# Two transformer layers on one core: interleaved MLP chains, two-bank exponentials in the last attention block, plain score maxima listed one unit later

## The chip, the cores and the metric

The kernel runs on one core of one Trainium2 chip. The metric is the device time of one execution in microseconds (us). The kernel before the change has a median of 3666.82 us in 3 runs (3660.86 to 3669.71).

## The reference

Two layers are computed on `x` of 2048 rows and 640 columns, in fp32. Each layer is an attention block (32 heads of 20) and an MLP (640 to 1536 to 640, squared relu), both with a layernorm in front and a residual behind. Both layers use the same weights.

```python
def _A_ref(x, wqkv, wo):
    qkv = (x @ wqkv).reshape(B, S, 3, H, Dh).transpose(2, 0, 3, 1, 4)
    q, k, v = qkv[0], qkv[1], qkv[2]
    scores = jnp.einsum("bhqd,bhkd->bhqk", q, k) * (Dh ** -0.5)
    p = _softmax(scores, axis=-1)
    o = jnp.einsum("bhqk,bhkd->bhqd", p, v)
    return o.transpose(0, 2, 1, 3).reshape(B, S, D) @ wo

def _B_ref(x, w1, b1, w2, b2):
    h = jnp.einsum("bsd,df->bsf", x, w1) + b1
    r = jnp.where(h > 0, h, 0)
    return jnp.einsum("bsf,fd->bsd", r * r, w2) + b2

x = x + _A_ref(_layernorm(x), wqkv, wo)
x = x + _B_ref(_layernorm(x), w1, b1, w2, b2)
x = x + _A_ref(_layernorm(x), wqkv, wo)
x = x + _B_ref(_layernorm(x), w1, b1, w2, b2)
```

## The kernel before

Every fp32 product is made of three products of rounded halves (`THREE`: high by high, high by low, low by high). A layer has three stages, and the program of each engine is written out by hand: engines work through their lists strictly in order and wait on semaphores, so the place of an instruction in its list decides what stands behind it while it waits.

**qkv.** The rows are taken in four blocks `tb` of 512. The projections to q and k come in 40 units: one unit is one chain of matmuls (L321 in `product`), worked as two half chains on the upper and the lower 64 rows of the array, 30 matmuls a unit. A finished chain is copied out by ACT, split into halves by POOL (`split_on_pool`), stored to DRAM (`d_qk`), and loaded again in the layout of the heads (`load_k`, `load_q`). The softmax needs the maximum of each row of scores. It is found beforehand, by matmuls of q with k (L473, `by_queries`) whose results DVE reduces (L485, "plain" maxima, listed in `PLAIN`) or whose pairs of key blocks are combined by ACT and DVE (L494 and L502, listed in `DOUBLE`, with the tiles `kd` of differences of keys). As many of these as fit are put between the projection matmuls; the rest is done in the attention stage. After each unit the counter `n` decides whether the loads of a group are issued (`tiles`) and whether its maxima are put on the list `groups`, from which `following` takes them.

**attention.** There are 32 blocks `t` of 512 queries by 4 heads, each with 16 units (`NKT`), a unit being 128 keys. A unit has four score matmuls into the four banks of `ps_st` (L555), four exponentials by ACT (L562, one bank of 512 columns each), and the product with v (L567, `pv`), whose eight matmuls (four heads, two passes) add to bank 7. Banks 4 to 6 belong to the maxima (L473). The strings in `ORDERS` give the order: a and b are scores, m and n maxima, V is `pv` of the oldest unit. In the last block no maxima are left, so only a, b and V do anything there.

**mlp.** After the output projection, each of four row blocks `qb` goes through two halves `fh` of the hidden width: six chains of the first product (L285, 512 columns wide) give six tiles `h` by ACT relu with bias (L1147), DVE square (L1148), ACT cast to the high half (L255) and DVE difference for the low half (L256). Then eight chains of the second product (L285, 320 columns) of 18 matmuls each run through the six tiles in order, and DVE adds each result to its rows (L1167). The line that builds a chain of the second product:

```python
                    chain(dst[:, :HALF], [
                        (hs[f % 6][:, hx, i * P : (i + 1) * P], w_2.piece(at_2(f, hw, hf)))
                        for f in range(fh * 6, fh * 6 + 6)
                        for hx, hw in THREE
                    ])
```

Of the kernel before, what the change touches and what calls it, by code (L numbers as in the profile page):

```python
# [10 lines left out]
AF = mybir.ActivationFunctionType  # L11
# [5 lines left out]
P = 128  # L17
# [22 lines left out]
def tile_layers(  # L40
# [11 lines left out]
    nc = tc.nc  # L52
# [17 lines left out]
    def dma(eng, dst, src):  # L70

        if dst.dtype == F32R:
            dst = dst.bitcast(F32)
        if src.dtype == F32R:
            src = src.bitcast(F32)
        eng.dma_start(dst, src)  # L76
# [4 lines left out]
    banks = psum.tile([P, 8, 512], F32, tag="banks", name="banks")  # L81
# [17 lines left out]
    ps_all = Ring(0, 1, 2, 3, 4, 5, 6, 7)  # L99
# [102 lines left out]
    w_2 = Split("w2", HALF, NF * 4)  # L202

    def at_2(f, hw, hf):

        return (((f // 6) * 2 + hf) * 6 + f % 6) * 2 + hw
# [75 lines left out]
    def chain(dst, pairs):  # L282
        last = len(pairs) - 1
        for n, (a, b) in enumerate(pairs):
            nc.tensor.matmul(dst, a, b, start=(n == 0), stop=(n == last))  # L285
# [387 lines left out]
    def qkv(first, x_src, rest):  # L673
# [41 lines left out]
        def tiles(x):  # L715
            g, qb, c = x
            for c in [c] if c in range(4) else [c, 2 * "de".index(c)]:
                if (g, c) not in k_t:
                    if c in range(4):
                        load_k(g, c, g > 1)  # L720
                    else:
                        load_kd(g, c)
            if g * NQB + qb not in q_t:
                load_q(g * NQB + qb)
# [159 lines left out]
        for j in range(len(chains)):  # L884
            if j < len(UNITS):
                while UNITS[min(j + 1, len(UNITS) - 1)][0] not in xt_:
                    step_rest()
                run(early, j)
            while min(at_now) < (j + 1) * N if j + 1 == len(chains) else at_now[0] < (j + 1) * N:
                for r in range(2):  # L890
                    if not insert(r):
                        work_on(r)
                now["pe"] += 0.235 if j < len(UNITS) else 0.155
                state["n"] += 1
                if state["n"] % 4 == 0 and not state["turn"]:
                    step_rest()
            if first:
                w_qk.save_full(1)
                w_v.save_full(1)
            if j < len(UNITS):  # L900
                run(late, j)
                later(1)
            n = j - 2
            if 1 < n < NQB * FIRST + 2:
                b, step = divmod(n - 2, 4)
                have, new = groups, PLAIN[b][step // 2]
                if step % 2:
                    have.extend(new)
                    soon[:] = [y for y in soon if y not in new]
                elif new:  # L910
                    tiles(new[0])
                    soon.append(new[0])
                if step == 2 and DOUBLE[b][0]:
                    tiles(DOUBLE[b][0][0])
                    soon.append(DOUBLE[b][0][0])
            if n in (10, 13, 17):
                b = n // 4 - 1
                double.extend(DOUBLE[b][0] + DOUBLE[b][1])
                coming[:] = [y for y in coming if y not in double]
                soon[:] = [y for y in soon if y not in double]  # L920
# [20 lines left out]
    def attention(first, x_src, first_rows):  # L941
# [59 lines left out]
        def op(o):  # L1001
            if o in "ab":
                par = "ab".index(o)
                i, p = divmod(st_n[par], 2)
                if i >= last:
                    return
                st_n[par] += 1
                if i > state["begun"]:
                    state["begun"] = i
                    begin(i)  # L1010
                score(i // NKT, i % NKT, 2 * p + par, es_of.setdefault(i, {}))
            elif o in "mn":
# [12 lines left out]
                smax(sm_ring, t, p, sub, c, par)  # L1025
                if n == ends[t] and min(sm_n) > n:
                    over.add(t)
                    if t * NKT > state["begun"] + 2 * NKT:
                        del q_t[t]
            else:  # L1030
                i = state["done"]
                if i >= last or min(st_n) < 2 * (i + 1):
                    return
                t, u = divmod(i, NKT)
                if u == 0:
                    state["acc"] = banks[:, 7, :]
                pv(state["acc"], t, u, es_of.pop(i))
                state["done"] += 1
                if u == NKT - 1:
                    steps = finish(t, state["acc"])  # L1040
                    split.update((i + j, f) for j, f in zip((4, 6, 7, 9, 11, 12), steps))
                t = rows["next"]
                if rows["at"] is not None:
                    if state["begun"] >= rows["at"]:
                        mrows_load(t)
                        rows.update(next=t + 1, at=None)
                elif t in over and t in q_t and state["begun"] >= (t - 2) * NKT + 4:
                    mrows_max(t)
                    mrows(t)
                    rows["at"] = state["begun"] + 2  # L1050

        def pairs():

            n, i = min(sm_n), state["begun"] + 1
            most = max(
                [8 * (e + 1 - n) / max(t * NKT - 5 - i, 1) for t, e in ends.items() if e >= n],
                default=0,
            )
            state["debt"] += most
            n = min(max(round(state["debt"]), 12), 16)  # L1060
            state["debt"] -= n
            return n

        for o in "abab":
            op(o)
        while state["done"] < last:
            for o in ORDERS[pairs()]:
                op(o)
        q_t.clear()
        k_t.clear()  # L1070
        v_t.clear()
# [60 lines left out]
    def mlp(qb, xnt, x_mid, x_dst, side):  # L1132

        xs = []
        for fh in range(2):
            hs = []
            for f in range(fh * 6, fh * 6 + 6):
                dst = ps_all("pu")
                chain(dst, [
                    (w_1.piece(f * 10 + hw * KD + k), xnt[k][:, hx, :])  # L1140
                    for k in range(KD)
                    for hw, hx in THREE
                ])
                if qb == NQB - 1:
                    w_1.past(f * 10 + 9)
                r = xtile("r")[:, :QB]
                nc.scalar.activation(r, dst, AF.Relu, bias=b1_t[:, f : f + 1])  # L1147
                nc.vector.tensor_mul(r, r, r)  # L1148
                h = slot([P, 2, QB], F32R, "h")
                split_to(h[:, 0, :], h[:, 1, :], r)  # L1150
                hs.append(h)
                if fh == 0 and f in (1, 2, 3, 4):
                    x = row_tile(x_mid, qb * 4 + f - 1)
                    nc.gpsimd.tensor_add(x, x, b2_t)
                    xs.append(x)
                side()
            for hf in range(2):
                c = slice(hf * HALF, (hf + 1) * HALF)
                for i in range(4):
                    dst = ps_all("y")  # L1160
                    chain(dst[:, :HALF], [
                        (hs[f % 6][:, hx, i * P : (i + 1) * P], w_2.piece(at_2(f, hw, hf)))
                        for f in range(fh * 6, fh * 6 + 6)
                        for hx, hw in THREE
                    ])
                    x = xs[i]
                    nc.vector.tensor_add(x[:, c], dst[:, :HALF], x[:, c])  # L1167
                    if fh == 1 and hf == 1:
                        r0 = (qb * 4 + i) * P
                        dma(nc.sync, x_dst[r0 : r0 + P, :], x)  # L1170
                    side()
            if fh == 0 and qb == NQB - 1:
                w_2.past(at_2(5, 1, 1))

# [169 lines left out]
```

## Time and profile before

| what | before |
|---|---|
| median of 3 runs | 3666.82 us (3660.86 to 3669.71) |
| the profiled execution's own time | 3667.64 us |
| its span, first to last instruction | 3665.0 us |
| mean granted TensorE clock | 0.996 |
| busy share of PE, DVE, ACT, POOL | 99%, 74%, 72%, 22% |
| layer 1: qkv, attention, output projection and mlp | to about 321, 1415 and 1845 us |
| layer 2: the same | to about 2152, 3241 and 3665 us |

A busy PE in this profile is not PE at its peak: the ends of matmuls are modelled, and an instruction whose start is held back can still leave the engine counted as busy. Waits are therefore read from the distance between starts and from the weight loads (PEld), which stand in the same list as the matmuls and wait for the same semaphores.

### The profile page before, as it was taken

The page shows a single profiled execution, that of the slowest core. Times are in us where ns is not written, and L with a number is a line of the kernel's source. Part 1 is how long each engine was busy: PE and PEld are TensorE (multiplying, and loading weights), DVE is VectorE, ACT ScalarE, POOL GpSimd, SP SyncE. Part 2 cuts the span into 40 slices and gives each one's busy share as a digit, 9 for nine tenths or more (in the row PEclk, how much of TensorE's full clock was granted, in tenths as well). Part 3 has the DMA queues.
Part 4 walks back from the last instruction along what each step waited for, and adds up shares of the span by engine and source line. Part 5 has one row for each costly group of instructions (what it writes and reads, how often), then busy time and mean ns, then how long its engine had stood idle before and what let it go on. Part 6 is the DMA issues. An engine that isn't in the chain of part 4 may idle for free.

```text
span 3665.0 us, 67658 instructions
## 1 busy us (share of the span) xinstructions
PE 3627.8 (99%) x25770; PEld 2165.3 (59%) x25770; DVE 2725.3 (74%) x5039; ACT 2645.5 (72%) x5199; POOL 819.1 (22%) x909
## 2 busy tenths in 40 slices
PE   8999999999999999999999999999999999999999
PEld 6896343333334336899878963333343433378998
DVE  7877999999999982344567779999999999723443
ACT  2778999999999994122217789999999999941221
POOL 6530433221221120111154202211211212101110
PEclk9999999999999999999999999999999999999999
DMA  7875555323221137411367652232232121373111
GB/s 262 286 233 170 167 149 155 102 68 79 56 49 44 50 104 241 155 44 44 101 229 244 219 151 75 69 78 55 71 76 58 47 52 42 110 258 132 44 51 36
DMA packets 255260, 426.50 MB, mean 116 GB/s; under 512 B 60444, under 2 KB 107292, under 8 KB 254936
## 3 DMA queue, kind: packets, MB, share of 16 engines
q1 hardware_dynamic: 254120, 419.83, 37.2%
q8 instruction: 202, 3.31, 0.4%
q10 hardware_dynamic: 816, 2.36, 0.2%
q14 instruction: 122, 1.00, 0.1%
HBM read 262.20 MB, written 159.88 MB: 115 GB/s over the span
## 4 chain that ended last, share of the span: by engine, by line
PE 95%; DVE 2%; ACT 1%; DMA 1%; POOL 1%; issue 0%; SPq 0%; ACTq 0%; DVEq 0%; POOLq 0%
PE banks L567 28%; PE banks L285 21%; PE banks L555 20%; PE banks L473 16%; PE banks L321 10%; DMA q<-d_qk 1%; DVE h L256 1%; PE banks L1121 0%; DVE r L1148 0%; ACT h L255 0%; PE banks L392 0%; DVE mx L485 0%; ACT r L1147 0%; DVE bst L243 0%; SPq L76 0%
## 5 line engine op out<-in xcount | busy, mean ns | idle before, releaser
L562 ACT ACTIVATE e<-banks 128x512 f32<-128x512 f32 x4096 | 2113.5, 604 | 66.1 <-PE banks L555 5.5
L485 DVE TENSOR_REDUCE mx<-banks 128x1 f32<-128x512 f32 x3068 | 1927.3, 684 | 218.2 <-PE banks L473 144.6
L473 PE MATMUL banks<-k,q 60*128 60x512 f32 x3583 | 1248.6, 429 | 12.4 <-DMA q<-d_qk 10.5
L555 PE MATMUL banks<-q,k 62*128 62x512 f32 x4096 | 1152.7, 435 | 0.9 <-ACT rl L494 0.5
L567 PE MATMUL banks<-e,vg 128*32 128x512 f32 x8192 | 1092.9, 605 | 0.0
L555 PEld LDWEIGHTS banks<-q,k 62*128 62x128 f32 x4096 | 600.1, 185 | 695.9 <-ACT e L562 664.2
L473 PEld LDWEIGHTS banks<-k,q 60*128 60x128 f32 x3583 | 583.0, 185 | 299.4 <-DVE mx L485 216.0
L502 DVE CUSTOM_DVE_ANT_0 rl<-banks,rl 128x512 f32<-128x512 f32 x515 | 335.8, 689 | 105.6 <-PE banks L473 93.7
L321 PE MATMUL banks<-xnT,wqk 64*128 64x512 f32 x2400 | 385.9, 399 | 3.5 <-DVE xnT L256 1.2
L567 PEld LDWEIGHTS banks<-e,vg 128*32 128x32 f32 x8192 | 161.6, 108 | 357.7 <-issue 332.3
L285 PE MATMUL banks<-w,h 128*128 128x320 f32 x2304 | 358.8, 312 | 7.5 <-DVE h L256 4.3
L285 PEld LDWEIGHTS banks<-w,h 128*128 128x128 f32 x2304 | 340.9, 189 | 17.0 <-DVE h L256 8.7
L494 ACT ACTIVATE rl<-banks 128x512 f32<-128x512 f32 x519 | 275.1, 597 | 96.8 <-PE banks L473 96.0
L285 PE MATMUL banks<-xnT,w 128*128 128x512 f32 x1440 | 330.0, 389 | 0.0
L1147 ACT ACTIVATE r<-banks,b_t 128x512 f32<-128x512 f32 x96 | 66.1, 689 | 360.0 <-PE banks L285 357.8
L321 PEld LDWEIGHTS banks<-xnT,wqk 64*128 64x128 f32 x2400 | 291.1, 189 | 36.5 <-ACT r L262 2.0
L285 PEld LDWEIGHTS banks<-xnT,w 128*128 128x128 f32 x1440 | 269.5, 188 | 55.1
L267 POOL CAST mr<-nt 128x32 fp32r<-128x32 f32 x64 | 13.4, 209 | 1172.7 <-DVE nt L528 1172.7
L611 POOL TENSOR_TENSOR few<-few,minus_t 128x16 f32<-128x16 f32 x62 | 179.8, 2900 | 199.6 <-DMA few<-d_s 199.6
L321 PE MATMUL banks<-wv,xnT 64*128 64x320 f32 x1920 | 198.9, 307 | 1.8 <-ACT mark_t L323 1.8
L1167 DVE TENSOR_TENSOR x<-banks,x 128x320 f32<-128x320 f32 x128 | 62.9, 492 | 183.3 <-PE banks L285 183.0
L255 ACT CAST xnT<-banks 128x512 fp32r<-128x512 f32 x70 | 39.9, 588 | 212.9 <-PE banks L1121 132.0
(77 smaller groups left out, 2104.1 us busy)
## 6 DMA issues: line engine op xcount, KB each, us to landing
q<-d_qk SPq DMA_DIRECT2D x248, 240.0 KB
d_qk<-ev SPq DMA_DIRECT2D x80, 512.0 KB
k<-d_qk SPq DMA_DIRECT2D x152, 240.0 KB
x<-d_x SPq DMA_DIRECT2D x88, 320.0 KB
d_qk<-ev SPq DMA_DIRECT2D x80, 256.0 KB
d_o<-ot SPq DMA_DIRECT2D x248, 80.0 KB
ot<-d_o SPq DMA_DIRECT2D x38, 512.0 KB
d_v<-v SPq DMA_DIRECT2D x32, 512.0 KB
```

What stands on the lines that cost most here:

```text
L285: nc.tensor.matmul(dst, a, b, start=(n == 0), stop=(n == last))
L321: m = nc.tensor.matmul(ch["dst"][:, :width], *pair, start=first, stop=last)
L473: nc.tensor.matmul(dst, q_t[t][b : b + 60, p, sub * P : (sub + 1) * P], k_t[t // NQB, c][b : b + 60, p, :], start=True, stop=True,)
L485: nc.vector.tensor_reduce(maxima(t)[:, 2 * par + p, sub, c : c + 1], dst, axis=AX.X, op=ALU.max)
L494: nc.scalar.activation(res, dst, AF.Relu)
L502: nc.vector.tensor_tensor_reduce(out=r, in0=dst, in1=r, scale=1.0, scalar=LEAST, op0=ALU.add, op1=ALU.max, accum_out=maxima(t)[:, 2 * par ...
L555: nc.tensor.matmul(dst, k_t[t // NQB, kt // 4][b : b + 62, p, (kt % 4) * P : (kt % 4 + 1) * P], q_t[t][b : b + 62, p, :], start=True, stop ...
L562: nc.scalar.activation(es[p][:, par, :], dst, AF.Exp, scale=SCALE)
L567: nc.tensor.matmul(acc[32 * h : 32 * h + 32, :], v_t[t // NQB, kt // 8][:, kt % 8, 32 * h : 32 * h + 32], es[p][:, par, :], start=(kt == 0 ...
L611: nc.gpsimd.tensor_tensor(few, few, minus_t, op=ALU.pow)
L1147: nc.scalar.activation(r, dst, AF.Relu, bias=b1_t[:, f : f + 1])
L1167: nc.vector.tensor_add(x[:, c], dst[:, :HALF], x[:, c])
```

## The change

Three edits that do not touch each other.

In the mlp, the first two chains of each second product are opened together: five sixths of the first, five sixths of the second, the last sixth of the first, the last sixth of the second, then both additions. The other six chains are as before.

In the last attention block of each layer (the units from `wide = last - NKT` on), `both_heads` writes the scores of a pair of heads into two neighbouring banks out of 0 to 5 and takes both with one exponential of 1024 columns. The order there is written anew: `pv` of a unit, then the second pair of the next unit and the first pair of the one after it.

In qkv, the maxima of a plain group are put on `groups` one unit later than before; the loads are issued where they were.

```diff
@@ qkv @@
-            if 1 < n < NQB * FIRST + 2:
-                b, step = divmod(n - 2, 4)
-                have, new = groups, PLAIN[b][step // 2]
-                if step % 2:
-                    have.extend(new)
-                    soon[:] = [y for y in soon if y not in new]
-                elif new:
-                    tiles(new[0])
-                    soon.append(new[0])
-                if step == 2 and DOUBLE[b][0]:
+            b, step = divmod(n - 2, 4)
+            if step % 2 == 0 and 0 <= b <= NQB:
+                if b < NQB and PLAIN[b][step // 2]:
+                    tiles(PLAIN[b][step // 2][0])
+                    soon.append(PLAIN[b][step // 2][0])
+                new = PLAIN[b][0] if step and b < NQB else PLAIN[b - 1][1] if not step and b else []
+                groups.extend(new)
+                soon[:] = [y for y in soon if y not in new]
+                if step and b < NQB and DOUBLE[b][0]:
                     tiles(DOUBLE[b][0][0])
                     soon.append(DOUBLE[b][0][0])
@@ attention @@
-                if i >= last or min(st_n) < 2 * (i + 1):
+                if i >= last or i < last - NKT and min(st_n) < 2 * (i + 1):
...
+        def both_heads(p):
+
+            i = state["wide"]
+            t, kt = divmod(i, NKT)
+            if p == 0 and i > state["begun"]:
+                state["begun"] = i
+                begin(i)
+            es = es_of.setdefault(i, {})
+            es[p] = weights[len(e_n) % len(weights)]
+            e_n.append(t)
+            state["bank"] = (state["bank"] + 2) % 6
+            dst = banks[:, state["bank"] : state["bank"] + 2, :]
+            for par in range(2):
+                b = 64 * par
+                nc.tensor.matmul(
+                    dst[:, par, :],
+                    k_t[t // NQB, kt // 4][b : b + 62, p, (kt % 4) * P : (kt % 4 + 1) * P],
+                    q_t[t][b : b + 62, p, :],
+                    start=True,
+                    stop=True,
+                )
+            nc.scalar.activation(es[p], dst, AF.Exp, scale=SCALE)
+            if p:
+                state["wide"] += 1
...
+        wide = last - NKT
+        state.update(wide=wide, bank=2)
+        spare = 0
+        while state["done"] < wide:
+            for o in ORDERS[pairs()]:
+                if o in "ab" and st_n["ab".index(o)] == 2 * wide:
+                    spare += 1
+                    if spare in (2, 4):
+                        both_heads(spare // 2 - 1)
+                else:
+                    op(o)
+        assert min(sm_n) == len(todo) and spare == 4
+        both_heads(0)
         while state["done"] < last:
-            for o in ORDERS[pairs()]:
-                op(o)
+            op("V")
+            for p in (1, 0):
+                if state["wide"] < last:
+                    both_heads(p)
@@ mlp @@
+            f0 = fh * 6
+
+            def part(dst, hf, i, fs):
+                for f in fs:
+                    for hx, hw in THREE:
+                        nc.tensor.matmul(
+                            dst[:, :HALF],
+                            hs[f][:, hx, i * P : (i + 1) * P],
+                            w_2.piece(at_2(f0 + f, hw, hf)),
+                            start=(f == 0 and (hx, hw) == THREE[0]),
+                            stop=(f == 5 and (hx, hw) == THREE[-1]),
+                        )
...
+            first_two = [ps_all("y") for _ in range(2)]
+            for fs in (range(5), (5,)):
+                for i in range(2):
+                    part(first_two[i], 0, i, fs)
+            for i in range(2):
+                add(first_two[i], 0, i)
             for hf in range(2):
-                c = slice(hf * HALF, (hf + 1) * HALF)
-                for i in range(4):
+                for i in range(0 if hf else 2, 4):
                     dst = ps_all("y")
...
+                    part(dst, hf, i, range(6))
+                    add(dst, hf, i)
```

Three places in PE's list show what moves; they are told here in the order of the argument. The first is in the last attention block of layer 1, near its end; `e` are the tiles of exponentials, `q`, `k`, `vg` those of the queries, keys and values. Before:

```order
L555 MATMUL banks<-q_14199,k_5403 128x512 x4
L567 MATMUL banks<-e_4758,vg_14075 32x512 x2
L567 MATMUL banks<-e_4757,vg_14075 32x512 x2
L555 MATMUL banks<-q_14199,k_5403 128x512 x4
L567 MATMUL banks<-e_4754,vg_14075 32x512 x2
L567 MATMUL banks<-e_4753,vg_14075 32x512 x2
```

The same place after the change:

```order
L1065 MATMUL banks<-q_14198,k_5402 128x512 x4
L567 MATMUL banks<-e_4750,vg_14074 32x512 x2
L567 MATMUL banks<-e_4749,vg_14074 32x512 x2
L1065 MATMUL banks<-q_14198,k_5402 128x512 x4
L567 MATMUL banks<-e_4752,vg_14074 32x512 x2
L567 MATMUL banks<-e_4751,vg_14074 32x512 x2
```

The rows look alike, but a row of four scores is another one: before, it is the whole of unit i+1, ahead of the product of unit i; now it is the second pair of unit i and the first pair of unit i+1, so the second pair of a unit stands behind the product of the unit before it.

The second place is the start of the second product in layer 1, on PE; `h` are the hidden tiles in the order of `f`, and the last of the six is h_16244 before and h_16211 now. Before, the first chain and the start of the second:

```order
L285 MATMUL banks<-w_15941,h_16196 128x320 x3
L285 MATMUL banks<-w_15941,h_16220 128x320
L285 MATMUL banks<-w_15943,h_16220 128x320
L285 MATMUL banks<-w_15941,h_16220 128x320
L285 MATMUL banks<-w_15943,h_16244 128x320 x3
L285 MATMUL banks<-w_15937,h_16119 128x320 x3
```

Now, from the same tile of the first chain to the last tile of both:

```order
L1201 MATMUL banks<-w_15908,h_16187 128x320
L1201 MATMUL banks<-w_15904,h_16086 128x320 x3
L1201 MATMUL banks<-w_15904,h_16115 128x320
L1201 MATMUL banks<-w_15906,h_16115 128x320
L1201 MATMUL banks<-w_15904,h_16115 128x320
L1201 MATMUL banks<-w_15906,h_16139 128x320 x3
L1201 MATMUL banks<-w_15908,h_16163 128x320 x3
L1201 MATMUL banks<-w_15908,h_16187 128x320
L1201 MATMUL banks<-w_15910,h_16187 128x320
L1201 MATMUL banks<-w_15908,h_16187 128x320
L1201 MATMUL banks<-w_15910,h_16211 128x320 x6
```

Fifteen matmuls of the second chain have moved ahead of the first use of the last tile, and nothing else stands between.

The third place is on PE in the qkv stage of layer 2, where the first group of maxima starts; `xnT` and `wqk` are the operands of the projections. Before, it stands behind the 180th projection matmul of the stage:

```order
L321 MATMUL banks<-xnT_18605,wqk_18682 128x512
L321 MATMUL banks<-xnT_18605,wqk_18719 128x512
L473 MATMUL banks<-k_19119,q_19122 128x512 x4
L321 MATMUL banks<-xnT_18535,wqk_18719 128x512
L321 MATMUL banks<-xnT_18535,wqk_18682 128x512
```

Now it stands behind the 210th:

```order
L321 MATMUL banks<-xnT_18572,wqk_18695 128x512
L321 MATMUL banks<-xnT_18572,wqk_18658 128x512
L473 MATMUL banks<-k_19086,q_19089 128x512 x4
L321 MATMUL banks<-xnT_18502,wqk_18658 128x512
L321 MATMUL banks<-xnT_18765,wqk_18620 128x512
```

One unit, 30 matmuls, has moved ahead of the group. Counted through the list in the same way, the later plain groups of layer 2 start at matmul 270 and 336 (before 240 and 306), the first use of a `kd` tile moves from 390 to 396, and in layer 1 the first group moves from 180 to 222 and the first `kd` from 398 to 390. Layer 1 fits as many maxima between its projections as before, layer 2 eight matmuls of maxima fewer, which are done in its attention stage.

More of the change, by code (lines that the diff above doesn't have):

```diff
@@ L1156, in mlp, with add @@
                 side()
+            f0 = fh * 6
[9 more added lines that the diff above has]
+                        )
+            def add(dst, hf, i):
+                c = slice(hf * HALF, (hf + 1) * HALF)
+                x = xs[i]
+                nc.vector.tensor_add(x[:, c], dst[:, :HALF], x[:, c])
+                if fh == 1 and hf == 1:
+                    r0 = (qb * 4 + i) * P
+                    dma(nc.sync, x_dst[r0 : r0 + P, :], x)
+                side()
+            first_two = [ps_all("y") for _ in range(2)]
[4 more added lines that the diff above has]
+                add(first_two[i], 0, i)
             for hf in range(2):
-                c = slice(hf * HALF, (hf + 1) * HALF)
-                for i in range(4):
+                for i in range(0 if hf else 2, 4):
                     dst = ps_all("y")
[L1161 to L1171, printed above, removed]
+                    part(dst, hf, i, range(6))
+                    add(dst, hf, i)
             if fh == 0 and qb == NQB - 1:
```

## The prediction

> **What bounds the kernel now.** I read the page first: the engines' busy time, then the chain that ended last.
>
> ```profile
> PE 3627.8 (99%) x25770; PEld 2165.3 (59%) x25770; DVE 2725.3 (74%) x5039; ACT 2645.5 (72%) x5199; POOL 819.1 (22%) x909
> PE 95%; DVE 2%; ACT 1%; DMA 1%; POOL 1%; issue 0%; SPq 0%; ACTq 0%; DVEq 0%; POOLq 0%
> ```
>
> TensorE is the bound nearly everywhere, so an edit is worth what PE waits at its place, or what it newly makes PE wait. All three edits touch PE's list, each in another stage, so I read each stage by itself: the table by stage around the last attention block, then timelines of PE and ACT.
>
> ```profile
> 1380.00:1390.00 10.00, 10.00 (x61) 3.29 (x60) 0.69 (x1) 9.94 (x20) 0.00 (x0) 1.00 0.35 114
> ...
> 1384.48 1.07 PE L567 MATMUL banks<-e,vg 128*32 128x512 f32 x8
> 1385.48 1.05 PE L555 MATMUL banks<-q,k 62*128 62x512 f32 x4
> ...
> 1386.01 0.60 ACT L562 ACTIVATE e<-banks 128x512 f32<-128x512 f32 x1
> ...
> 1414.55 0.15 PEld L567 LDWEIGHTS banks<-e,vg 128*32 128x32 f32 x6 [0.56 <-ACT e L562]
> ```
>
> In the stretch 1380 to 1390 of the first of these tables DVE has nothing left (0.69) and ACT is busy 9.94 of 10.00: the last block is held by exponentials. Its first product starts at 1384.48 and its last at 1414.55: 15 steps in 30.07 us, 2.00 us a unit.
>
> The profiled execution took 3667.64 us, 0.8 above the median of the runs shown (3666.82); the sum is made against it. About 0.3% (11 us) is what a measurement can tell from no change.
>
> **The change part by part. The mlp chains.** The weight loads show the wait, in the table of waits and in PE's timeline:
>
> ```profile
> PEld banks L285 <- DVE h L256: 8.7, 17, 1.6
> PEld banks L285 <- ACT h L255: 7.1, 15, 2.1
> ...
> 1552.98 2.94 PE L285 MATMUL banks<-w,h 128*128 128x320 f32 x17
> 1556.10 3.05 PE L285 MATMUL banks<-w,h 128*128 128x320 f32 x19 [0.17 <-DVE h L256]
> ...
> 1559.58 2.65 PE banks L285 x18
> ...
> 1770.86 2.57 PE L285 MATMUL banks<-w,h 128*128 128x320 f32 x15
> 1775.26 0.56 PE L285 MATMUL banks<-w,h 128*128 128x320 f32 x2 [1.83 <-ACT h L255]
> 1775.99 5.32 PE L285 MATMUL banks<-w,h 128*128 128x320 f32 x24 [0.17 <-DVE h L256]
> ...
> 1776.20:1779.70 3.50, 3.50 (x15) 3.50 (x15) 1.49 (x4) 0.00 (x0) 0.74 (x2) 0.51 0.33 96
> ```
>
> 18 matmuls run in 2.65 us, 0.147 each. In an ordinary first chain the eighteenth starts 1556.10 - 1552.98 = 3.12 after the first instead of 17 x 0.147 = 2.50: 0.6 lost, on the high half of the last tile and then on its low half. There are 32 such waits, two in each of the 16 first chains (2 layers, 4 row blocks, 2 halves), 8.7 + 7.1 = 15.8 us together. The dearest one is followed by a stretch at 0.51 of the clock: 24 matmuls take 5.32 instead of 3.5, 1.8 more. At stake: 17.6 us. The edit puts 15 matmuls, 2.2 us, in front of the first use of the last tile. The longest wait, 2.1, fits under that; behind it the low half comes 0.73 after the high one (1775.99 against 1775.26), so some 0.5 stays there. **Gain 17 us, 15 to 17.6.** What hides the conversions afterwards is the second chain; without it the 0.7 of each chain would be back. The additions of the two chains come together, a chain later, into a ring of eight banks with six free: nothing.
>
> **The plain maxima.** PE waits for q tiles in DRAM:
>
> ```profile
> PE banks L473 <- DMA q<-d_qk: 11.1, 4, 4.1
> ...
> 42.95 7.55 DMA q<-d_qk
> 80.27 7.84 DMA q<-d_qk
> 1870.18 4.87 DMA q<-d_qk
> 1894.29 5.29 DMA q<-d_qk
> ...
> 50.50:60.00 9.50, 9.41 (x52) 7.19 (x54) 5.46 (x9) 2.06 (x4) 5.04 (x6) 0.71 0.84 288
> 1875.00:1882.00 7.00, 6.81 (x43) 5.86 (x45) 5.81 (x10) 0.14 (x1) 2.62 (x3) 0.76 0.95 347
> 1900.00:1908.00 8.00, 8.00 (x46) 6.81 (x47) 5.36 (x9) 0.67 (x2) 0.81 (x2) 0.63 1.00 316
> ```
>
> The four waits end 4.9 to 7.8 us after the issue of the load. Three are plain groups; the short one, at 88.1, is for a `kd` group, whose list the edit leaves alone. Behind each long wait the clock falls: 9.5 x 0.29 + 7 x 0.24 + 8 x 0.37 = 7.4 us more. At stake: 11.1 + 7.4 = 18.5. Thirty projection matmuls, a whole unit, now cover each group; the waits themselves should go. But the loads that follow keep their own pace, and PE reaches them earlier. In layer 2:
>
> ```profile
> 1904.13 0.78 SPq L76 DMA_DIRECT2D q<-d_qk  x2
> ...
> 1895.60 0.82 PE L321 MATMUL banks<-xnT,wqk 64*128 64x512 f32 x4
> 1899.71 0.76 PE L473 MATMUL banks<-k,q 60*128 60x512 f32 x1 [3.29 <-DMA q<-d_qk]
> ...
> 1914.71 0.39 PE L473 MATMUL banks<-kd,q 60*128 60x512 f32 x1
> ...
> 1880.62 5.57 DVE mx L485 x9
> ```
>
> The third plain group would start at 1896.4 instead of 1899.71. From there to the first `kd` maximum it was 84 projection matmuls in 15.0 us, 12.0 without the slow clock; now it is 60, so 8.6: PE is there at 1905.0. Its q pair was issued at 1904.13. SP takes it in order behind stores of evictions that now run about 4.3 earlier (the first stall of 3.2 and part of its slow stretch, for which DVE, on the chain from 1880.62, had become the pace), so 1899.8, and lands up to 7.84 later, the longest of the four rows, since the DMA share there is 1.00: 1907.7. A wait of 2.7 comes back, with even odds of a slow window of 1.7. Of the 11.1 at stake in layer 2 (3.2 + 3.3 + 1.7 + 3.0, rounded) 1.7 was hidden behind DVE, 2.7 + 0.9 come back: 5.8. In layer 1, 4.1 + 2.8 = 6.9 are at stake and the 80.27 load returns about 2 in the same way: 5. **Gain 10.8 us**; 18.5 if no later load is late, 5 if they all are. Eight maxima matmuls move from one PE-bound stage to another: nothing.
>
> **The last block.** In the order now, the product of unit i stands ahead of the second pair of scores of unit i+1, whose exponential the product of unit i+1 waits for. That is a closed loop: exponential ends, product, scores, exponential. ACT has only the first pair of unit i+1 queued meanwhile. Before, all four scores of unit i+1 stood ahead of the product of unit i. The loop's terms: 0.05 from the end of an exponential to the product (the ACT row that ended at 1414.50 and the load at 1414.55, below), 1.00 from product to scores (1384.48 to 1385.48), 0.53 from scores to exponential (1385.48 to 1386.01), and one exponential of 1024 columns, which no row shows:
>
> ```profile
> 1411.42 3.08 ACT L562 ACTIVATE e<-banks 128x512 f32<-128x512 f32 x6
> ...
> L562 ACT ACTIVATE e<-banks 128x512 f32<-128x512 f32 x4096 | 2113.5, 604 | 66.1 <-PE banks L555 5.5 <-PE banks L473 4.8
> L262 ACT COPY r<-banks 128x512 f32<-128x512 f32 x82 | 47.8, 587 | 47.2 <-PE banks L392 19.4 <-PE banks L321 17.7 <-PE banks L473 6.7
> L367 ACT COPY v<-banks 128x320 f32<-128x320 f32 x64 | 27.0, 426 | 10.8 <-PE banks L321 6.9 <-PE banks L473 3.6
> ...
> 1379.84 10.21 ACT L562 ACTIVATE e<-banks 128x512 f32<-128x512 f32 x20
> ```
>
> Copies from banks of 512 and 320 columns differ by 161 ns, 0.84 a column, so 604 + 430 = 1.03 us. From above, 20 back-to-back exponentials in 10.21 bound the second half by 0.51: 1.11; from below, 0.60 and the 0.51 less the 0.1 by which two of them overlap: 1.01, and as no row has two banks I allow 0.95. I take 1.03, since the copies read the same banks. The loop is 0.05 + 1.00 + 0.53 + 1.03 = 2.61 a unit; 15 x 2.61 = 39.2 against 30.07, and the first product starts some 0.2 earlier, an estimate, since both its pairs are scored ahead and only the copy of bank 7 still holds it: 8.9 a layer. **Loss 17.8 us**, 15.4 to 20.2. The exponentials that ACT saves are off this loop.
>
> Sum: 3667.64 - 17.0 - 10.8 + 17.8 = 3657.6 us, 0.27% below, inside the 0.3%.
>
> **The rivals.**
>
> ```profile
> 2151.70:2155.10 3.40, 3.25 (x15) 1.39 (x11) 1.68 (x4) 3.17 (x8) 0.00 (x0) 1.00 0.39 158
> 2155.10:2158.60 3.50, 3.50 (x17) 1.35 (x15) 1.90 (x6) 2.28 (x6) 0.46 (x2) 0.51 0.36 106
> 3336.10:3339.50 3.40, 2.06 (x13) 1.53 (x11) 2.59 (x2) 0.71 (x2) 3.40 (x3) 1.00 0.41 154
> ...
> 2155.14 1.93 PE L567 MATMUL banks<-e,vg 128*32 128x512 f32 x8
> 2157.00 0.79 PE L555 MATMUL banks<-q,k 62*128 62x512 f32 x1
> 2157.83 1.57 ACT L562 ACTIVATE e<-banks 128x512 f32<-128x512 f32 x3 [1.22 <-PE banks L473]
> ```
>
> *The clock falls in the last block* (slower). The new loop has 12 matmuls in 2.61 us, 15.6 in 3.4. For: a stretch with 15 score matmuls was followed by clock 0.51. Against: one with 13 full-height ones, as the products are, was not. [...] At half clock a product takes 1.86 to the scores and these 0.83 to the exponential: a loop of 3.77, 26.3 us a layer more than before, 3692; with every second window slow 3675. The Trainium skill, "TensorE: Matmul & The Clock Gate", section "A second HAM failure mode: psum-queue depth-cycling", says that micro-idles of PE between groups, with banks cycled each time, make the clock oscillate: it speaks against this change; the row at 2155.10 agrees that short gaps can do it. Chance 0.17.
>
> *ACT's rate is the pace* (faster). If the loop did not close, each pair would cost 1.03 less the overlap of 0.1 and a unit 1.88 instead of 2.00: 3.7 us gained, 3636. For: ACT is busy 9.94 of 10. Against: the order. The Trainium skill, "ScalarE: Activation LUTs", section "What ACT_TABLE_LOAD costs", gives an exponential 186 ns and 0.833 a column, with 93 of overlap; by that rule alone two banks in one instruction save time, and no run here shows a wide one yet. Chance 0.07.
>
> *The qkv edit gains nothing*, every later load being as late as the one removed: 3668. For: DMA share 1.00. Against: 30 matmuls of cover at three places. Chance 0.08.
>
> **How the numbers follow.** My case has 0.68. Its own range is 3667.64 - 17.6 - 18.5 + 15.4 = 3647 to 3667.64 - 15 - 5 + 20.2 = 3668; its middle lies 1 us inside the 0.3% line, so I split it 0.29 faster, 0.39 same. The clock rival gives 0.10 slower, 0.07 same; ACT's rate 0.07 faster; the late loads 0.08 same. Together 0.36, 0.54, 0.10. The range 3647 to 3676 takes in my case, the late loads and the half-slow clock, 0.81.
>
> **What would show it.** Right: products in the last block 2.6 us apart, ACT idle in each unit behind PE, wide exponentials of about 1.03; no wait of PEld for `h` above some tenths; the three q waits gone and one for `kd` grown near 1905. Wrong: products 2.0 or less apart, a granted clock below 1.00 in the last blocks, or waits for q of the old length in qkv.

## The result and the profile after

| | before | after |
|---|---|---|
| median, with lowest and highest | 3664.18 us (3660.86 to 3673.78, 12 runs) | 3659.1 us (3657.65 to 3663.07, 12 runs) |
| profiled execution's own time | 3667.64 us | 3659.64 us |
| its span | 3665.0 us | 3657.8 us |

The ratio after to before is 0.9984 (95% interval 0.9975 to 0.9993). That is a fall of 2.6 to 9.2 us, inside the 0.3% that the prediction counted as no change. The forecast was 3657.6.

The first two lines are the busy time and the chain that ended last on the page of after; the others are its groups of instructions by line (idle time in front of the group, and what ended it, behind the last bar).

```profile
PE 3604.9 (99%) x25770; PEld 2153.4 (59%) x25770; DVE 2725.1 (75%) x5039; ACT 2645.2 (72%) x5131; POOL 819.4 (22%) x909
PE 95%; DVE 2%; ACT 2%; POOL 1%; issue 0%; DMA 0%; SPq 0%; ACTq 0%; DVEq 0%; POOLq 0%
...
L567 PE MATMUL banks<-e,vg 128*32 128x512 f32 x8192 | 1091.8, 605 | 29.7 <-ACT e L1072 28.8 <-DVE o L580 1.0
L1201 PEld LDWEIGHTS banks<-w,h 128*128 128x128 f32 x2304 | 339.3, 188 | 2.5 <-DVE h L256 1.3
L1072 ACT ACTIVATE e<-banks 128x1024 f32<-128x1024 f32 x64 | 62.3, 1021 | 22.7 <-PE banks L1065 22.4
```

Three things moved. DMA went from 1% of the chain to 0%: of PE's waits for q tiles, 11.1 us before, one of 2.0 is left. The weight loads of the second product (L1201 now, L285 before) wait 1.3 us for `h`, all of it for DVE, where it had been 8.7 for DVE and 7.1 for ACT. And there are two new waits in the last block: PE stands 28.8 us behind the wide exponential (L1072), and that exponential 22.4 us behind the scores (L1065). Two engines that wait for each other in turn are a closed loop.

The chain of waits in the last block of layer 1 shows that loop, piece by piece (start, duration, what):

```profile
1394.35 1.03 ACT e L1072
1395.38 0.04 issue
1395.42 1.06 PE banks L567 x8
1396.49 0.45 PE banks L1065 x2
1396.94 0.02 issue
1396.96 0.02 ACTq L1072
1396.98 0.04 issue
1397.02 1.03 ACT e L1072
```

From one wide exponential that a product waits for to the next it is 1397.02 - 1394.35 = 2.67 us, unit after unit, where it was 2.00 by the prediction's count. The table by stage over the last block has the clock at 1.00 throughout, while ACT, which had 9.94 of 10 before, falls below:

```profile
1380.00:1390.00 10.00, 7.65 (x50) 2.04 (x48) 0.69 (x1) 8.19 (x12) 0.00 (x0) 1.00 0.31 97
1390.00:1400.00 10.00, 6.91 (x48) 1.82 (x48) 0.00 (x0) 7.06 (x9) 2.90 (x1) 1.00 0.54 160
```

From the starts of the first and last projection matmul (L321) and the last product (L567), and to the end of the span for the last mlp, the stages took:

| stage | layer 1, before to after | layer 2, before to after |
|---|---|---|
| qkv | 304.9 to 305.9 (+1.0) | 306.2 to 293.3 (-12.9) |
| attention | 1094.3 to 1103.5 (+9.2) | 1089.2 to 1100.3 (+11.1) |
| output projection and mlp | 430.4 to 421.6 (-8.7) | 424.3 to 417.3 (-6.9) |

The sum is -7.2 us, the difference of the spans. Three terms of 10 to 20 us of both signs leave almost nothing; whether each is what the prediction said it is was the question of the experiments.

### The profile page after: what moved, and what is told of

The parts are those of the page before. It is cut to its first block, busy times and chain, and to the rows that moved or that the text cites. A ratio compares the mean times of both kernels' runs of the same rounds, so it can differ in the third digit from the quotient of the medians.

```text
span 3657.8 us, 67630 instructions
## 1 busy us (share of the span) xinstructions
PE 3604.9 (99%) x25770; PEld 2153.4 (59%) x25770; DVE 2725.1 (75%) x5039; ACT 2645.2 (72%) x5131; POOL 819.4 (22%) x909
## 4 chain that ended last, share of the span: by engine, by line
PE 95%; DVE 2%; ACT 2%; POOL 1%; issue 0%; DMA 0%; SPq 0%; ACTq 0%; DVEq 0%; POOLq 0%
PE banks L567 28%; PE banks L555 19%; PE banks L473 16%; PE banks L285 12%; PE banks L321 10%; PE banks L1201 9%; ACT e L1072 1%; PE banks L1160 0%; DVE mx L485 0%; PE banks L392 0%; PE banks L1065 0%; ACT e L562 0%; DVE bst L243 0%; DVE h L256 0%; DMA q<-d_qk 0%
## 5 line engine op out<-in xcount | busy, mean ns | idle before, releaser
L562 ACT ACTIVATE e<-banks 128x512 f32<-128x512 f32 x3968 | 2049.5, 604 | 65.7 <-PE banks L473 6.8
L567 PE MATMUL banks<-e,vg 128*32 128x512 f32 x8192 | 1091.8, 605 | 29.7 <-ACT e L1072 28.8
L555 PE MATMUL banks<-q,k 62*128 62x512 f32 x3968 | 1118.1, 434 | 1.0 <-DVE mx L502 0.3
L555 PEld LDWEIGHTS banks<-q,k 62*128 62x128 f32 x3968 | 583.8, 185 | 657.3 <-ACT e L562 625.3
L502 DVE CUSTOM_DVE_ANT_0 rl<-banks,rl 128x512 f32<-128x512 f32 x511 | 333.6, 689 | 102.3 <-PE banks L473 93.5
L567 PEld LDWEIGHTS banks<-e,vg 128*32 128x32 f32 x8192 | 161.2, 108 | 389.9 <-issue 324.8
L321 PE MATMUL banks<-xnT,wqk 64*128 64x512 f32 x2400 | 382.8, 396 | 3.4 <-DVE xnT L256 1.2
L1201 PE MATMUL banks<-w,h 128*128 128x320 f32 x2304 | 349.4, 310 | 0.8 <-DVE h L256 0.7
L494 ACT ACTIVATE rl<-banks 128x512 f32<-128x512 f32 x515 | 273.6, 598 | 101.5 <-PE banks L473 93.3
L1201 PEld LDWEIGHTS banks<-w,h 128*128 128x128 f32 x2304 | 339.3, 188 | 2.5 <-DVE h L256 1.3
L285 PE MATMUL banks<-xnT,w 128*128 128x512 f32 x1440 | 330.0, 389 | 0.0
L321 PEld LDWEIGHTS banks<-xnT,wqk 64*128 64x128 f32 x2400 | 289.3, 187 | 37.9 <-issue 2.3
L285 PEld LDWEIGHTS banks<-xnT,w 128*128 128x128 f32 x1440 | 269.6, 188 | 55.1
L321 PE MATMUL banks<-wv,xnT 64*128 64x320 f32 x1920 | 199.7, 307 | 0.9 <-ACT mark_t L323 0.9
L321 PEld LDWEIGHTS banks<-wv,xnT 64*128 64x128 f32 x1920 | 187.9, 185 | 2.6 <-ACT mark_t L323 1.6
```

Of the source, the lines that this page charges most:

```text
L321: m = nc.tensor.matmul(ch["dst"][:, :width], *pair, start=first, stop=last)
L494: nc.scalar.activation(res, dst, AF.Relu)
L502: nc.vector.tensor_tensor_reduce(out=r, in0=dst, in1=r, scale=1.0, scalar=LEAST, op0=ALU.add, op1=ALU.max, accum_out=maxima(t)[:, 2 * par ...
L555: nc.tensor.matmul(dst, k_t[t // NQB, kt // 4][b : b + 62, p, (kt % 4) * P : (kt % 4 + 1) * P], q_t[t][b : b + 62, p, :], start=True, stop ...
L562: nc.scalar.activation(es[p][:, par, :], dst, AF.Exp, scale=SCALE)
L567: nc.tensor.matmul(acc[32 * h : 32 * h + 32, :], v_t[t // NQB, kt // 8][:, kt % 8, 32 * h : 32 * h + 32], es[p][:, par, :], start=(kt == 0 ...
```

## The experiments

All ratios are to the kernel before on the same chip; each kernel ran 4 to 11 times beside 6 to 15 runs of before.

### Each edit alone

Three kernels keep one edit each and take the other two back. For the last block:

> Only the edit of the last attention block, the rest as before. Theory (the order closes a loop of 2.67 us a unit, and the three edits add up): 10 us a layer lost, 19 to 20 us slower than before, ratio 1.0053, products 2.67 us apart. Rival (the edits interact: the last block is late because the output projection or the mlp behind it starts with other buffers): the loss comes out other than 19 by more than 4 us.

Measured: 3686.01 against 3666.49 us, ratio 1.0056 (1.0043 to 1.0068): 19.5 slower, products 2.67 apart. For the mlp:

> Only the interleaved chains of the mlp, the rest as before. Theory (the 15 matmuls, 2.2 us, of the second chain cover the conversion of the last tile h): the waits of PEld for h fall from 15.8 us to under 4, and the time falls by 14 to 17 us, ratio 0.9955 to 0.9965. Rival (part of what the mlp stages gained in after came from the other edits, for instance from the tail of the last block): the gain is under 11 us.

Measured: 3650.82 against 3666.08, ratio 0.9955 (0.9943 to 0.9967): 15.3 faster. The group of the weight loads:

```profile
L1162 PEld LDWEIGHTS banks<-w,h 128*128 128x128 f32 x2304 | 339.3, 188 | 1.7 <-DVE h L256 0.6
```

For the plain maxima:

> Only the plain maxima a unit later, the rest as before. Theory (three q waits and the slow clock behind them go; the gain is what the prediction put at 10.8): 8 to 13 us faster than before, ratio 0.9965 to 0.998; the profile shows layer 1's stage shorter by some 3 to 5 us wherever the slow stretch of the clock at its start is as short as before (3.4 us), and equal where it is long. Rival (layer 1 gains nothing because the waits moved to the normalising of its rows): layer 1's stage equal at any start, layer 2's shorter by 12.

Measured: 3653.82 against 3666.49, ratio 0.9966 (0.9954 to 0.9979): 12.7 faster. Layer 2's qkv stage took 293.5 us instead of 306.2, the 12 of the rival. Layer 1's took 305.4 instead of 304.9, but these two don't compare: both profiles have a stretch of half clock of some 3.5 us near the start, in before from 11.5 to 15.0, ahead of its first projection matmul at 15.8, here from 15.9 on, inside the stage. Sorted by that over all profiles, layer 1's stage takes 304.9 and 305.0 with the old lists and 303.7 with those of the change where the half clock lies ahead of it, and 306.4 and 307.0 against 304.4 to 305.9 where 3.3 to 4.2 us of it lie inside. So layer 1 gains about 1.3 us: less than the 3 to 5 of the theory, more than the nothing of the rival.

The three medians add up to 19.5 - 15.3 - 12.7 = -8.5; the whole change measured 0.9984 of 3664, -5.9, with an interval of -9.2 to -2.6. The edits add up within what the runs can tell.

### Order or width in the last block

The change did two things there: another order, and one exponential for two banks. Two kernels separate them. The first keeps the order and goes back to 512 columns:

```diff
-            nc.scalar.activation(es[p], dst, AF.Exp, scale=SCALE)
+            for par in range(2):
+                nc.scalar.activation(es[p][:, par], dst[:, par], AF.Exp, scale=SCALE)
```

> As after, but each pair of banks in the last block is taken by two exponentials of 512 columns instead of one of 1024; the order stays as after. Theory (the order, product of unit i ahead of the second scores of unit i+1, closes the loop): products stay 2.5 to 2.8 us apart, and the time stays within 5 us of after, ratio to before 0.997 to 1.0005. Rival (the wide exponential is what costs, since it waits for both banks and holds both): products go back to 2.0 apart and the time falls to some 19 us below after, ratio 0.993.

Measured: 3659.21 us, ratio 0.9982 (0.9974 to 0.9991), as after. The chain of waits of this kernel has the same loop; ACT's rest (the group's idle time) is behind the scores here too:

```profile
1394.92 1.07 PE banks L567 x8
1395.98 0.71 PE banks L1065 x4
...
1397.00 0.60 ACT e L1073
1397.60 0.04 issue
1397.64 1.06 PE banks L567 x8
...
L1073 ACT ACTIVATE e<-banks 128x512 f32<-128x512 f32 x128 | 66.2, 603 | 20.5 <-PE banks L1065 20.3
```

1397.64 - 1394.92 = 2.72 us a unit. The second kernel keeps the wide exponential and puts the second pair of scores of the next unit ahead of the product again:

```diff
+            if state["wide"] < last:
+                both_heads(1)
             op("V")
-            for p in (1, 0):
-                if state["wide"] < last:
-                    both_heads(p)
+            if state["wide"] < last:
+                both_heads(0)
```

> As after, wide exponentials included, but in the last block the second pair of scores of unit i+1 stands ahead of the product of unit i, as before the change. Theory (order): the loop is open, ACT always has two wide exponentials queued, products 1.9 to 2.1 us apart at ACT's rate (two rows of two wide exponentials show 1.94 us), so 9 to 12 us a layer less than after, 18 to 24 in all: 3635 to 3641, ratio to before 0.992 to 0.994. Rival (the wide exponential costs): products stay at 2.5 or more and the time within 5 us of after, ratio 0.997 to 1.000.

Measured: 3631.94 against 3666.49 us, ratio 0.9907 (0.9892 to 0.9923), 27 us below the median of after and 3 below the range of the theory. From 1387 to 1409 its chain of waits has no piece of PE any more, and the wide exponentials rest for 0.3 us in all 64 together:

```profile
1394.26 0.86 ACT e L1072
1395.12 0.04 issue
1395.17 0.19 ACT e L1072
1395.36 0.73 issue
1396.09 0.87 ACT e L1072
...
L1072 ACT ACTIVATE e<-banks 128x1024 f32<-128x1024 f32 x64 | 59.3, 1078 | 0.3
```

1396.09 - 1394.26 = 1.83 us a unit, two wide exponentials of 0.92. (The theory's 1.94 is a pair up to the end of its second one; in a row they start 0.92 apart.) In the order of the change the width hardly matters (2.67 and 2.72); with the wide exponential the order alone makes 2.67 or 1.83. The wide exponential is a gain that the order had buried: 1.83 against 2.04 in before, where the products that start at 1384.48 and 1413.00 are 14 units apart. That is before's four exponentials of 0.51; the prediction's 2.00 counts the last product at its second half, at 1414.55. The fall of 27 us is 0.84 x 15 = 12.6 a layer, 25 in all, and about 2 that these runs don't resolve.

### How much cover the mlp needs

Only one part of the second chain, instead of five, stands ahead of the first use of the last tile:

```diff
-            for fs in (range(5), (5,)):
-                for i in range(2):
-                    part(first_two[i], 0, i, fs)
+            for i, fs in ((0, range(5)), (1, (0,)), (0, (5,)), (1, range(1, 6))):
+                part(first_two[i], 0, i, fs)
```

> As the kernel with only the mlp edit, but only one part (3 matmuls, 0.44 us) of the second chain stands ahead of the first use of the last tile h, instead of five. Theory (the gain is the cover, matmul for matmul): each of the 16 first chains wins at most 0.44 us, together 7 us, ratio 0.998 (0.9972 to 0.9988); waits of PEld for h of about 9 us stay. Rival (any break between the chains is enough, since the wait is only a hand-over of a semaphore): 13 us or more, ratio under 0.9967.

Measured: 3658.62 against 3666.08, ratio 0.9981 (0.9973 to 0.999), 7.5 us faster, with 6.5 and 1.7 of the waits left:

```profile
L1162 PEld LDWEIGHTS banks<-w,h 128*128 128x128 f32 x2304 | 339.3, 188 | 9.3 <-DVE h L256 6.5 <-ACT h L255 1.7
```

0.44 us of cover in 16 chains gave 7, 2.2 us gave 15: the gain is the work put in front, until the wait is used up. Three chains instead of two, on the kernel with the open loop:

```diff
-            first_two = [ps_all("y") for _ in range(2)]
+            first_two = [ps_all("y") for _ in range(3)]
...
-                for i in range(2):
+                for i in range(3):
```

> The kernel with the second pair of scores ahead of the product and wide exponentials, and in the mlp three chains instead of two share their first five parts (30 matmuls, 4.4 us, in front of the first use of the last tile). Theory (the cover of 2.2 us already hides nearly all; 3.8 us of weight loads' waits for h are left in after): 0 to 4 us less than with two chains, 3628 to 3632, ratio 0.9900 to 0.9912. Rival (three additions that come together hold the ring of banks or DVE): slower by 3 us or more.

Measured: 3630.82 against 3666.08, ratio 0.9903 (0.989 to 0.9917), 1.1 below the kernel with two chains. That is less than these runs resolve: no harm, and hardly anything left to cover. The 3.8 of the theory was read wrongly: in the row of L1201 above, 2.5 is the whole idle time and the 1.3 for `h` is part of it.

### The wait that is left in layer 1's qkv

In after, one wait for q is left in qkv, at 86 us, for a `kd` group. The list of these groups is put off by a unit too:

```diff
-            if n in (10, 13, 17):
+            if n in (11, 14, 18):
```

> The kernel with the second pair of scores ahead of the product, and in qkv the maxima of the kd groups too are listed a unit later, loads where they were. Theory (the one q wait that is left in qkv, 2.0 us at 86 in layer 1, is a load that is late for its place): that wait goes, 1 to 3 us less, 3629 to 3631, ratio 0.9900 to 0.9910. Rival (in layer 1 the pace is set elsewhere, by how the half-height matmuls pair up and by the normalising of the rows, so a removed wait is given back): layer 1's qkv stage within 1 us of that of the kernel without this edit.

Measured: 3633.49 us, ratio 0.9912 (0.9898 to 0.9926), 1.5 above the kernel without it, so no gain. Both theories missed. The wait went and layer 1's qkv stage became 5.0 us shorter (304.4 to 299.4), a part of it because here the half clock lies ahead of the stage. But layer 1's attention took 1.9 more, with a stretch of half clock of 3.4 us at 318.6, just behind the qkv stage, and in layer 2 four more matmuls of maxima (575 in qkv, where it had been 579) went to the attention stage, which took 2.6 more: the starts of its products fall back in three steps of 1.7 to 1.8, where without this edit there is one of 1.3. Layer 2's qkv stage took 1.7 more as well (293.0 to 294.7). So the last kernel puts the `kd` groups off in layer 1 alone, with three chains in the mlp:

> The kernel with three interleaved chains and the second pair of scores ahead of the product, and the kd groups listed a unit later in layer 1 alone (in both layers, layer 1's qkv stage was 4.8 us shorter, and layer 2's attention stage 2.6 longer in steps of 1.7, where maxima that no longer fitted into qkv are done). Theory (the loss is the maxima pushed out of layer 2's qkv, the gain is layer 1's q wait and the better pairing of half-height matmuls): layer 1's qkv stage 4 to 5 us shorter than with the lists of the change, layer 2 unchanged: 3626 to 3628, ratio 0.9888 to 0.9897. Rival (layer 1's gain is a chance of the clock at its start): 3630 to 3633, ratio 0.9902 to 0.991.

Measured: 3628.98 against 3669.65 us, ratio 0.9888 (0.987 to 0.9906). This is the lowest median of all kernels run here, though the interval overlaps that of the kernel with three chains. Layer 1's qkv stage is 4.4 us shorter than with three chains alone (303.7 to 299.3), as the theory said, and layer 2 unchanged. The rival's clock is not the reason: the half clock lies ahead of the stage in the slower one and reaches some 3 us into it in the faster one. Yet attention in layer 1 again took 2.3 more, behind a stretch at half clock in the table by stage:

```profile
319.00:322.40 3.40, 3.40 (x16) 1.23 (x15) 1.67 (x5) 2.10 (x5) 0.46 (x2) 0.51 0.43 124
```

So 3628.98 lies between the two expectations in time; by the ratio, against a before that was 3.6 slower here, it lies at the edge of the theory's. Such a stretch between 318 and 327 is in the profiles of five kernels (the last block alone, the two with the mlp edit alone, and the two of this section), and in none of the other six. What sets it off stays open.

## Why the prediction was right, point by point

**The last block** was forecast at +17.8 (15.4 to 20.2): the edit alone cost 19.5, and in the change the last block, from the start of its first product matmul to that of its last, takes 10.0 us more in layer 1 and 9.9 in layer 2 (forecast 8.9). The mechanism is shown: the order closes the loop, whatever the width. The row of chain pieces has all four terms: 0.04 for 0.05, 1.06 with 0.45 and the hand-over to 1397.02 for 1.00 + 0.53, and 1.03 for the exponential that no row had shown. The loop is 0.06 longer than the 2.61 of the sum: 15 x 0.06 = 0.9 a layer, nearly all that is missing; and the first product, which was to start 0.2 earlier, starts 0.13 and 0.02 nearer to the one before it. The 0.06 lies between product and exponential: from 1395.42 to 1397.02 they are 1.60, not 1.00 + 0.53. The rows at 1396.94 to 1397.02 show where: in front of the wide exponential ACT's queue takes a step of its own (ACTq, an instruction for a semaphore), 0.08 from the end of the scores to its start. The 0.53 had been read from an exponential of before, which has no such step. It doesn't come with the width: the kernel with 512 columns and the new order has 116 such steps for its 128 exponentials of one bank.

**The mlp** was forecast at -17.0 (15 to 17.6): -15.3 alone, -15.6 by the stages of the change. The step is right, matmul for matmul, as the short cover shows. The one term that was a size too big is the slow clock of 1.8 behind the longest wait. It is in before's profile but not in that of the kernel with the qkv edit alone, whose layer 1 stage took 428.5 instead of 430.4 with the old chains: a chance of that execution.

**The plain maxima** were forecast at -10.8 (5 to 18.5) and gave -12.7 alone, -11.9 by the stages; but the sum was right with two wrong halves. Layer 1 was to win 5 and won about 1.3 (in this pair of profiles it lost 1.0), layer 2 was to win 5.8 and won 12.9. That the sum came out is luck.

*Layer 2.* Two terms of the prediction failed here. "2.7 + 0.9 come back": the q pair for the `kd` group, and PE's first matmul of that group, in the timelines of SP and PE of after:

```profile
1899.79 0.94 SPq L76 DMA_DIRECT2D q<-d_qk  x2
...
1907.10 0.47 PE L473 MATMUL banks<-kd,q 60*128 60x512 f32 x1 [0.34 <-DVE mx L485]
```

The issue came at 1899.8 as forecast. The load was nearly as slow as forecast too: its semaphore was complete at 1906.96, 7.2 us after the issue, and DVE's maxima, for which the same matmul waited, came 0.1 later. What failed is the place of PE: the prediction had it there at 1905.0, but the matmul before starts at 1906.37, and with 0.23 from one pair to the next this one would have started near 1906.6. Some 0.5 us came back, not 2.7, and no slow stretch. And "1.7 was hidden behind DVE": the first 180 projection matmuls of layer 2 took 31.0 us before and 26.2 after, 4.8 less, so the 3.2 of the stall and nearly all of its slow stretch went.

*Layer 1.* The table by stage of the projection matmuls alone (L321), cut so that each row holds the same matmuls before and after (the second counter, of weight loads, counts them). Before:

```profile
15.83:23.60 7.77, 7.21 (x60) 5.76 (x62) 1.00 0.89 315
23.60:51.85 28.25, 16.09 (x122) 11.20 (x121) 0.95 0.66 228
51.85:64.70 12.85, 10.04 (x62) 7.37 (x63) 0.84 0.65 207
64.70:86.35 21.65, 21.65 (x152) 18.84 (x150) 1.00 0.89 282
86.35:121.30 34.95, 33.50 (x212) 25.94 (x209) 1.00 0.94 331
121.30:221.60 100.30, 98.44 (x602) 73.86 (x600) 1.00 0.84 287
```

After:

```profile
15.88:25.55 9.67, 9.12 (x60) 7.25 (x62) 0.78 0.73 249
25.55:48.30 22.75, 15.91 (x126) 11.37 (x124) 1.00 0.59 209
48.30:62.65 14.35, 8.74 (x62) 5.94 (x60) 0.88 0.86 274
62.65:86.45 23.80, 21.86 (x154) 18.26 (x150) 1.00 0.97 296
86.45:120.45 34.00, 33.39 (x210) 25.94 (x211) 1.00 0.91 321
120.45:222.70 102.25, 100.52 (x603) 73.36 (x600) 1.00 0.81 279
```

The first row lost 1.9 where the edit changes nothing: the half clock, which in after reaches to 20.1 and in before ends at 15.0 (granted 0.78 against 1.00 in the row). It starts between 9.8 and 16.1 in the eleven profiles, whatever the kernel: a chance of the execution. The second row won 5.5: the stall of 4.1 and part of its slow stretch. The third gave back 1.5: PE, earlier now, runs into the normalising of its rows (first line below), and the slow stretch of the clock comes all the same. The fourth gave back 2.15, the 2 that the prediction had for the load at 80.27 (second line, the waits of PE in layer 1's qkv):

```profile
PE banks L392 <- DVE x L251: 2.4, 3, 1.0
PE banks L473 <- DMA q<-d_qk: 2.0, 1, 2.0
```

The fifth row won 0.95, and the sixth lost 1.95 at full clock. The same 600 projection matmuls and 240 of the maxima run there. They fill half of the array's rows each and run in pairs, two starts within 0.05 us; in this row 396 starts were the second of such a pair before, 377 in after, 403 in the fastest kernel, which took 99.95. The matmuls hardly wait there, but their weight loads do: for banks that ACT (L494) or DVE (L502) has yet to empty. The waits of PEld in the sixth row, before and then after:

```profile
PEld banks L473 <- DVE mx L502: 3.8, 16, 0.9
PEld banks L473 <- ACT rl L494: 3.7, 19, 0.2
...
PEld banks L473 <- ACT rl L494: 5.6, 30, 0.2
PEld banks L473 <- DVE mx L502: 4.1, 20, 0.8
```

Over the same stretch (from the 601st to the 1201st projection matmul), both layers of all eleven profiles fall into two groups: with 19 to 21 waits for ACT it took 99.9 to 100.8 us, with 28 to 30 it took 102.0 to 102.3. In layer 2 these are 28 waits and 102.1 us before, 21 and 100.8 after. Where the lists are the same, the times of a layer agree within 0.4 us. So the prediction left out a term of about 2 us of either sign: the order of the list decides how often a matmul of the maxima meets a bank that is not yet free. That the time follows the list and goes with these waits is shown; that they are the cause, by breaking pairs, was not tried. The number of pairs alone does not tell the time: 366 went with 100.8 us in layer 2 of after, 377 with 102.2 in layer 1.

"Eight maxima matmuls move: nothing" was 1.3 too low. In layer 2's attention the starts of the products fall back by 1.3 us in one step, about two fifths through, in every kernel with the qkv edit except the one that puts off the `kd` groups of both layers (three steps), and in none without.

**The base.** The sum was made against an execution of 3667.64, 3.5 above the median of the 12 runs of before. Forecast and median of after agree to 1.5 us, but the change is smaller than forecast: 5.1 by the medians, not 10.0. The close agreement in time is luck in part. By the edits' own medians the three terms, -27.8 + 17.8 in the forecast, were -28.0 + 19.5.

**The rivals.** *The clock falls in the last block*: it did not, 1.00 in the two rows of the result. The Trainium skill, "TensorE: Matmul & The Clock Gate", section "A second HAM failure mode: psum-queue depth-cycling", tells of a kernel whose clock oscillated under short idle times of PE between groups of matmuls. This trace does not agree: PE stood about 0.95 us in each unit of 2.67 and kept its clock. Nor does the prediction's row at 2155.10 bear the rule out: PE was busy 3.25 of 3.40 us in the row ahead of it, so the row doesn't show idle time as what halved the clock. *ACT's rate is the pace*: false for the change, and true as soon as the order is put back. The 1.88 that this rival gave a unit was measured as 1.83. The Trainium skill, "ScalarE: Activation LUTs", "What ACT_TABLE_LOAD costs", gives 186 ns and 0.833 a column, so by estimate 1039 ns for a lone wide exponential, and with the 93 of overlap 946 in a row; the chain of after has 1.03 us for one, and that of the open loop 0.92 in a row. *The qkv edit gains nothing*: false in sum, nearly true of layer 1.

## What to carry to other kernels

With queues worked in order, write down for each wait what stands behind it, and ask whether the thing waited for needs that in turn: a loop over two engines costs its whole length a unit, and here a different instruction inside it changed 0.05 us, one step of lookahead 0.84. A wide instruction that saves issue time shows its gain only where its engine is the pace, so test order and width apart. An early arrival at one wait is worth only what the next wait doesn't take back: follow a moved list to the end of its stage, and into the next one, before summing.

## What the runs showed of the hardware that was not expected

The same 840 half-height matmuls of two kinds took 99.9 to 102.3 us at full clock, depending on their order in the list and in step with how often (19 to 30 times) a weight load stood 0.2 us for a bank. A wide exponential over two banks costs 0.92 us in a row, a tenth less than two narrow ones (20 in 10.21, 0.51 each). A loop with 12 matmuls in 2.67 us and gaps of nearly 1 us kept the full clock, while the start of attention in layer 1 fell to half clock for 3.4 us in five of eleven profiles; why is open.
